# An FFT and mixture-of-experts kernel: scatters of the first segment 0.6 steps later, a scratch clear behind late scatters, and the routing copy on GpSimd

## The chip, the cores and the metric

The kernel runs on one core of a Trainium2 chip. The metric is the device time of one execution in microseconds (us); the time before is the median of three runs. Engine names are those of the profile: PE is TensorE's matmul, PEld its weight load, DVE is VectorE, ACT is ScalarE, POOL is GpSimd, SP is SyncE.

## The reference

The input x has 8 sequences of 2496 rows of 256 channels. Each channel of each sequence goes through a circular convolution, done in the frequency domain; then each of the 19,968 rows goes to the one of 8 experts whose gate logit is the largest, and comes back weighted with its gate probability.

```python
X = np.fft.rfft(x, axis=1)
Y = X * (filt_r + 1j * filt_i)[None]
x = np.fft.irfft(Y, n=2496, axis=1).reshape(8 * 2496, 256)
logits = x @ w_gate                          # 8 experts
expert_idx = np.argmax(logits, axis=1)
gate_w = softmax(logits)[arange(N), expert_idx]
for e in range(8):
    xe = x[expert_idx == e]
    h = np.maximum(xe @ w1[e], 0.0)          # 256 -> 1024
    out[expert_idx == e] = gate_w[...] * (h @ w2[e])   # 1024 -> 256
```

## The kernel before

The transform is done by matrix products. A sequence is two units of 128 channels, a unit is five steps: 80 steps in all. A step transposes (`spec1`), multiplies with a table (`spec2`), multiplies with the filter on DVE (`filt_`, tiles tr and ti), adds the two halves (`join`, on POOL up to step 70 and on DVE behind it) and multiplies back (`spec3`) into the buffer U.

When both units of a sequence b are through, the gate logits and the place of every row in its expert's list are worked out (`route1` to `route6`; the place is the tile dest, gate value and row number the tile meta). The rows are turned back into time in 11 pairs of groups of 117 rows: `inv1` and `inv2` make a tile yt of two groups by 260 columns. 256 of them are data, written by ACT (line 651); the last four are copied from meta by DVE (line 658, in `inv3`). Then POOL scatters each group into the list xs in HBM with one indirect DMA (line 158, in `scatter`). That makes 22 scatters a sequence, 176 in all. yt has five buffers.

The experts then work on blocks of 128 rows of xs, in three segments. The first has 16 blocks in 8 units and takes full blocks of the sequences up to b = 5, so it runs beside the last two sequences' inverse; the second has 48 blocks and waits for all scatters, and the rest is the third. A block b is loaded by SP (`load`), scaled and split into two f16 halves (`prep`, `split`), transposed by a DMA of SP (`turn`), and multiplied with both layers (`layer1`, `halves`, `layer2`, PE lines 1083 and 1109). ACT writes the result into ot (`out_`, four buffers), and POOL scatters it to the output (`send`, again line 158). At the end of the dispatch eight scatters of constant rows (`tail`) close the lists.

The order of the work on every engine is written out by hand. Each call is put into a list with a key in steps (`at`), the list is sorted by key, and the calls are made in that order; an engine does its instructions in the order in which they were made. A scatter has one of eight semaphores in turn, so it also waits until the scatter eight before it has landed. The key of `send` for a block of the first segment is 0.95 dx + 0.5 behind the start of the next block, where dx is the distance of two blocks: (90.5 - 80.9) / 16 = 0.6 steps.

Of the kernel before, what the change touches and what calls it, by code (L numbers as in the profile page):

```python
# [9 lines left out]
F32 = mybir.dt.float32  # L10
# [11 lines left out]
S, D, E, F = 2496, 256, 8, 1024  # L22
# [91 lines left out]
def tile_fft_moe(ctx, tc, x, filt_r, filt_i, w_gate, w1, w2, cst, out):  # L114
    nc = tc.nc
    B = x.shape[0]
# [7 lines left out]
    SEG = []  # L124
# [14 lines left out]
    cp = ctx.enter_context(tc.tile_pool(name="cp", bufs=1))  # L139
    ident = cp.tile([128, 128], F32, name="ident")  # L140
    small = cp.tile([128, 64], F32, name="small")
    zrow = cp.tile([128, ROW], F32, name="zrow")
    rbase = cp.tile([128, E], F32, name="rbase0")
    tbs = [cp.tile([128, 4], I32, name=f"tb{i}") for i in range(len(SEG))]
    nblk = cp.tile([128, 1], I32, name="nblk")
# [3 lines left out]
    def free(inst, own, *others):  # L149
        ins = inst.ins  # L150
        for g in (*others, own):
            tc.declare_no_dep(ins, group=g, reason="every row is written once")
        tc.add_to_no_dep_group(own, ins)
        writers.setdefault(own, []).append(ins.name)

    def scatter(dst, idx, src, bound, *groups):
        free(
            nc.gpsimd.indirect_dma_start(  # L158
                out=dst,
                out_offset=bass.IndirectOffsetOnAxis(ap=idx, axis=0),  # L160
                in_=src,
                in_offset=None,
                bounds_check=bound,
                oob_is_err=False,
            ),
            *groups,
        )

    def after(ins, names):
        for name in names:  # L170
            tc.add_manual_dep(
                ins,
                name,
                mybir.DependencyInfo(
                    mybir.DependencyClass.Sync, mybir.DependencyReason.DATA
                ),
                reason="the rows are dispatched",
            )
# [6 lines left out]
    with ExitStack() as fctx:  # L185
# [468 lines left out]
        def inv3(b, j, gg):  # L654
            yt = sti[b, j] if gg == 0 else sti.pop((b, j))
            dest, meta = rst[b]
            if gg == 0:
                nc.vector.tensor_copy(yt[:, :, D:], meta[:, 2 * j : 2 * j + 2])
            g = 2 * j + gg
            scatter(  # L660
                xs[:, :], dest[:, g : g + 1], yt[:, gg], E * NP - 1,
                f"s{b}", "ld", *(f"s{i}" for i in range(b)),
            )

        def blocks(rb, up, nm):

            t8 = lambda n, dt=F32: rp.tile([128, E], dt, name=nm + n, tag="t" + n)
            ci = t8("ci", I32)
            nb = t8("nb")
            nc.vector.tensor_tensor(nb, rb, small[:, 0:8], op=ALU.subtract)  # L670
            nc.vector.tensor_scalar(ci, nb, up, None, op0=ALU.add)
            nc.vector.tensor_scalar(ci, ci, 7, None, op0=ALU.arith_shift_right)
            nc.vector.tensor_copy(nb, ci)
            return nb
# [152 lines left out]
        def at(key, f, *a):  # L827
            work.append((key, f, a))
# [14 lines left out]
        def tail(e):  # L843
            scatter(
                xs[:, :], rst["tail"][:, e : e + 1], zrow, E * NP - 1,
                "z", "ld", *(f"s{i}" for i in range(B)),
            )


        K = {"s2": 1.394, "sr": 1.65, "si": 1.85, "s3": 3.6, "f": 0.063, "fd": 0.75, "w": 6.0, "wp": 4.1}  # L850
# [29 lines left out]
        for b in range(B):  # L880
# [26 lines left out]
            for j in range(NPAIR):  # L907
                z = s0 + lead + j * d
                at(z, inv1, b, j)
                at(z + 0.7 * c, inv2, b, j)  # L910
                z = max(z + 1.2 * c, s0 + c * RT[9] + 0.1 + 0.9 * d * j)
                for gg in range(2):
                    at(z + 0.45 * d * gg, inv3, b, j, gg)
# [9 lines left out]
            if b == B - 1:  # L923
                at(last + 0.1, tails)
                for e in range(E):
                    at(last + 1.2 + e, tail, e)
# [27 lines left out]
        home = []  # L954
# [173 lines left out]
        def send(b):  # L1128
            ot, t = st.pop(b)
            scatter(out[:, :], t, ot, N - 1, "out")  # L1130

# [33 lines left out]
        for b in range(NB):  # L1167
            z, d, s = tau[b]
            y = max(opened(s) + 0.3, z - (1.1 if b else 1.45))
            at(y, prep, b)  # L1170
            at(y + 0.05, split, b)
            at(y + 0.1, turn, b)
            at(z, layer1, b, 0)
            at(z + 0.2 * d, halves, b, 0)
            at(z + 0.25 * d, layer1, b, 1)
            at(z + 0.45 * d, halves, b, 1)
            nx, dx = (tau[b + 1][0], tau[b + 1][1]) if b + 1 < NB else (z + d, d)
            at(nx + 0.5 * dx, layer2, b, 0)
            at(nx + 0.75 * dx, layer2, b, 1)
            at(nx + 0.95 * dx, out_, b)  # L1180
            at(nx + 0.95 * dx + 0.5, send, b)
        for _, f, a in sorted(work, key=lambda w: w[0]):
            f(*a)

# [2 lines left out]
        with tc.If(n > NFIN - NREST):  # L1187
            for k in range(nu, len(units)):
                load(k)
                loadw(k, 0)  # L1190
                loadw(k, 1)
            for b in range(NB, NBLK):
                prep(b)
                split(b)
                turn(b)
            for b in range(NB, NBLK):
                for i in range(2):
                    layer1(b, i)
                    halves(b, i)
            for b in range(NB, NBLK):  # L1200
                layer2(b, 0)
                layer2(b, 1)
                out_(b)
                send(b)
# [32 lines left out]
```

## Time and profile before

| | |
|---|---|
| time, median of three runs | 1393.22 us (1393.07 to 1394.41) |
| time of the profiled execution | 1391.01 us |
| its span | 1389.2 us |
| PE busy | 1313.8 us (95%) |
| PEld busy | 1177.2 us (85%) |
| DVE busy | 831.5 us (60%) |
| ACT busy | 842.3 us (61%) |
| POOL busy | 470.7 us (34%) |

The span is what the profile shows between the first and the last instruction; 1.8 us of the profiled execution lie around it. Up to about 472 us the steps of the transform run, up to about 580 us the last two sequences are turned back beside the first segment, and behind about 608 us PE does expert blocks alone. A timeline row tells an instruction's start, its length, and in brackets how long its engine was idle before it and what ended that; "issue" means that the profile shows nothing that it waited for. The granted clock is given as a share of TensorE's full clock of 2.4 GHz; at 0.5 it is at its lower level of 1.2 GHz.

### The profile page before, as it was taken

Reading aid. Unit: us, or ns where it says so; the run is one execution under the profiler, and the core shown is the slowest. Engines: PE = TensorE matmul, PEld = TensorE weight load, DVE = VectorE, ACT = ScalarE, POOL = GpSimd, SP = SyncE. Lnnn points to the kernel's source line nnn. Section 1 sums busy time; section 2 is a strip of 40 time slices with the busy share of each in tenths; the row PEclk is TensorE's granted clock in tenths of the full one; section 3 lists DMA queues with packets and bytes.
Section 4 is the critical chain, followed back from the end, with each engine's and each line's share of the span. In section 5 each row is a group of like instructions: output and inputs, shape, how many; then the busy total and the mean of one; then the engine's idle time right before and its main releaser. Section 6 shows DMA issues by size and latency. Waiting matters only on the chain.

```text
span 1389.2 us, 38966 instructions
## 1 busy us (share of the span) xinstructions
PE 1313.8 (95%) x14855; PEld 1177.2 (85%) x14855; DVE 831.5 (60%) x2400; ACT 842.3 (61%) x1444; POOL 470.7 (34%) x446
## 2 busy tenths in 40 slices
PE   6799999999989899899999999999999999999997
PEld 5778777777877677789999999889999999999997
DVE  1698879888887464255555555555555555555552
ACT  3567667676766555455666665556656565656564
POOL 3638576485664433323111111111111111111111
PEclk9999999999999999999999999999999999999999
DMA  9746565565542722496878878573554546373731
GB/s 173 200 158 206 167 195 178 162 210 171 184 144 81 177 76 79 142 302 172 221 211 212 221 200 248 140 190 73 151 118 106 166 103 167 77 196 73 192 79 43
DMA packets 201438, 220.95 MB, mean 159 GB/s; under 512 B 104359, under 2 KB 177690, under 8 KB 190178
## 3 DMA queue, kind: packets, MB, share of 16 engines
q1 hardware_dynamic: 181310, 175.21, 45.9%
q0 software_dynamic: 19472, 42.51, 12.1%
q8 instruction: 118, 1.93, 0.6%
q10 hardware_dynamic: 468, 0.72, 0.2%
q14 instruction: 70, 0.57, 0.1%
HBM read 335.66 MB, written 61.56 MB: 286 GB/s over the span
## 4 chain that ended last, share of the span: by engine, by line
PE 48%; DMA 5%; issue 2%; DVE 1%; ACT 1%; SPq 1%; POOL 0%; POOLq 0%; ACTq 0%
PE ph L1083 24%; PE po L1109 24%; DMA wb<-wscr 3%; DMA wa<-wscr 1%; DVE bm L1097 1%; DMA T<-xs 0%; POOL out_dram L158 0%; ACT hs L1089 0%; ACT T L1091 0%; DMA xb<-xs 0%; DVE m L1048 0%; ACT xs L1062 0%; SPq L1070 0%; SPq L973 0%; DVE xs L1063 0%
## 5 line engine op out<-in xcount | busy, mean ns | idle before, releaser
L1083 PE MATMUL ph<-T,wa 128*128 128x128 f16 x7728 | 463.8, 220 | 14.1 <-issue 7.4
L1083 PEld LDWEIGHTS <-wa 128*128 128x128 f16 x7728 | 447.5, 98 | 27.2 <-issue 15.6
L1109 PE MATMUL po<-wb,T 128*128 128x256 f16 x2576 | 433.6, 274 | 6.6 <-DMA wb<-wscr 3.6
L1097 DVE TENSOR_TENSOR bm<-hs,T 128x512 f16<-128x512 f32 x322 | 222.7, 692 | 352.8 <-ACT T L1091 308.1
L158 POOL DMA_INDIRECT out_dram<-ot,t x161 | 157.2, 977 | 649.0 <-DVE xs L1063 567.1
L1109 PE MATMUL po<-wb,bm 128*128 128x256 f16 x1288 | 352.2, 273 | 0.0
L1109 PEld LDWEIGHTS <-T 128*128 128x128 f16 x2576 | 246.3, 98 | 38.2 <-issue 7.5
L1089 ACT ACTIVATE hs<-ph 128x512 f32<-128x512 f32 x322 | 191.6, 595 | 104.5 <-PE ph L1083 77.0
L158 POOL DMA_INDIRECT xs<-yt,dest x176 | 186.3, 1059 | 149.8 <-issue 45.7
L1062 ACT ACTIVATE xs<-xb,s 128x256 f16<-128x256 f32 x161 | 81.8, 508 | 226.3 <-DVE s L1052 224.0
L1091 ACT CAST T<-hs 128x512 f16<-128x512 f32 x322 | 199.0, 618 | 10.1
L1109 PEld LDWEIGHTS <-bm 128*128 128x128 f16 x1288 | 126.5, 98 | 15.2
L356 POOL TENSOR_TENSOR p<-tr,ti 128x512 f32<-128x512 f32 x71 | 95.4, 1344 | 85.2 <-DVE ti L348 78.3
L372 ACT COPY U<-pi 128x512 f32<-128x512 f32 (+1 forms) x80 | 87.4, 1093 | 48.9 <-PE pi L367 41.7
L1063 DVE SCALAR_TENSOR_TENSOR xs<-xb,s,xs 128x256 f16<-128x256 f32 x161 | 78.0, 485 | 59.3 <-ACT xs L1062 57.5
L649 PE MATMUL py<-gh,dm 117*117 117x512 f32 x176 | 94.0, 615 | 7.2 <-ACT gh L640 6.8
L367 PE MATMUL pi<-cm,p 128*128 128x128 f32 (+1 forms) x640 | 86.9, 279 | 10.3 <-POOL p L356 7.2
L264 PE MATMUL f<-a,x 117*128 117x117 f32 (+1 forms) x628 | 87.3, 277 | 5.6 <-DVE T L272 2.9
L327 PEld LDWEIGHTS px<-z,bm 128*128 128x128 f32 x640 | 80.0, 193 | 14.2 <-issue 11.5
L367 PEld LDWEIGHTS pi<-cm,p 128*128 128x128 f32 x640 | 79.0, 193 | 12.9 <-POOL p L356 7.9
L272 ACT COPY T<-f 128x468 f32<-128x468 f32 (+1 forms) x80 | 70.7, 884 | 30.5 <-PE f L264 28.8
L327 PE MATMUL px<-z,bm 128*128 128x128 f32 x640 | 87.1, 279 | 0.4 <-ACT U L372 0.4
(180 smaller groups left out, 1326.5 us busy)
## 6 DMA issues: line engine op xcount, KB each, us to landing
wb<-wscr SPq DMA_DIRECT2D x129, 1040.0 KB
wa<-wscr SPq DMA_DIRECT2D x129, 1024.0 KB
xb<-xs SPq DMA_DIRECT2D x161, 130.0 KB
wf<-in_moe_w_dram SPq DMA_DIRECT2D x32, 512.0 KB
x<-in_x_dram SPq DMA_DIRECT2D x210, 78.0 KB
wscr<-wh SPq DMA_DIRECT2D x8, 1040.0 KB
wscr<-wh SPq DMA_DIRECT2D x8, 1024.0 KB
xs<-yt,dest POOLq DMA_INDIRECT x176
```

Of the source, the lines that this page charges most:

```text
L158: nc.gpsimd.indirect_dma_start(out=dst, out_offset=bass.IndirectOffsetOnAxis(ap=idx, axis=0), in_=src, in_offset=None, bounds_check=bound, ...
L264: nc.tensor.matmul(ps[:, n : n + m], lhsT=xt.pop((u, g))[:m], rhs=a1[:m, :m], start=True, stop=True,)
L327: nc.tensor.matmul(ps[:, kk], lhsT=bm[:, 4 * it + kk], rhs=z[:, kk], start=True, stop=True,)
L356: e.tensor_tensor(p, tr, ti, op=ALU.add)
L367: nc.tensor.matmul(ps[:, o : o + n], lhsT=p[:, kk], rhs=cm[:, k, :n], start=True, stop=True)
L372: nc.scalar.copy(U[u % NU].rearrange("p n r -> p r n")[:, r0 : r0 + o // 64, :], ps[:, :o].rearrange("p (r n) -> p r n", n=N2),)
L649: nc.tensor.matmul(ps[:GP], lhsT=dm, rhs=gh[:GP], start=True, stop=True)
L1083: nc.tensor.matmul(ps[:, f], lhsT=w[:, p : p + 128], rhs=xt[:, r, c], start=(n == 0), stop=(n == 5))
L1089: nc.scalar.activation(s, ps, AF.Relu, scale=1.0 / B23)
L1091: nc.scalar.copy(hh, s)
L1097: nc.vector.tensor_tensor(hl, s, hh, op=ALU.subtract)
L1109: nc.tensor.matmul(ps, lhsT=h2[q][:, f % 4], rhs=wv[:, r, f], start=(f == 0 and n == 0), stop=(f == 7 and n == 2),)
```

## The change

A scratch tile `pad` of 128 x 384 f32 is added, and a function `pause` in which POOL clears it. It is called behind every scatter of the last two sequences (44), behind the eight scatters of `tail`, and behind the 16 scatters of the first segment's blocks: 68 times. The copy of the four routing columns into yt goes from DVE to POOL (88 times). The key of `send` for the first segment's blocks is 1.1 in place of 0.5, which is one block later.

```diff
--- before.py
+++ after.py
@@ -140,6 +140,7 @@
     ident = cp.tile([128, 128], F32, name="ident")
     small = cp.tile([128, 64], F32, name="small")
     zrow = cp.tile([128, ROW], F32, name="zrow")
+    pad = cp.tile([128, 384], F32, name="pad")
     rbase = cp.tile([128, E], F32, name="rbase0")
     tbs = [cp.tile([128, 4], I32, name=f"tb{i}") for i in range(len(SEG))]
     nblk = cp.tile([128, 1], I32, name="nblk")
@@ -165,6 +166,9 @@
             ),
             *groups,
         )
+
+    def pause():
+        nc.gpsimd.memset(pad, 0.0)
 
     def after(ins, names):
         for name in names:
@@ -655,12 +659,14 @@
             yt = sti[b, j] if gg == 0 else sti.pop((b, j))
             dest, meta = rst[b]
             if gg == 0:
-                nc.vector.tensor_copy(yt[:, :, D:], meta[:, 2 * j : 2 * j + 2])
+                nc.gpsimd.tensor_copy(yt[:, :, D:], meta[:, 2 * j : 2 * j + 2])
             g = 2 * j + gg
             scatter(
                 xs[:, :], dest[:, g : g + 1], yt[:, gg], E * NP - 1,
                 f"s{b}", "ld", *(f"s{i}" for i in range(b)),
             )
+            if b >= B - 2:
+                pause()
 
         def blocks(rb, up, nm):
 
@@ -845,6 +851,7 @@
                 xs[:, :], rst["tail"][:, e : e + 1], zrow, E * NP - 1,
                 "z", "ld", *(f"s{i}" for i in range(B)),
             )
+            pause()
 
 
         K = {"s2": 1.394, "sr": 1.65, "si": 1.85, "s3": 3.6, "f": 0.063, "fd": 0.75, "w": 6.0, "wp": 4.1}
@@ -1128,6 +1135,8 @@
         def send(b):
             ot, t = st.pop(b)
             scatter(out[:, :], t, ot, N - 1, "out")
+            if home[b][0] < SEG[0][2]:
+                pause()
 
 
 
@@ -1178,7 +1187,7 @@
             at(nx + 0.5 * dx, layer2, b, 0)
             at(nx + 0.75 * dx, layer2, b, 1)
             at(nx + 0.95 * dx, out_, b)
-            at(nx + 0.95 * dx + 0.5, send, b)
+            at(nx + 0.95 * dx + (1.1 if home[b][0] < SEG[0][2] else 0.5), send, b)
         for _, f, a in sorted(work, key=lambda w: w[0]):
             f(*a)
```

PE, ACT and SP have the same instructions in the same order. DVE loses the 88 copies and keeps the order of the rest. On POOL 88 copies and 68 clears are added, and the output scatters stand elsewhere. The line numbers of the changed kernel are 1 to 9 higher.

POOL, where the sequence b = 6 begins to be scattered (yt6_0 is its first pair of groups, xs_57 the list in HBM). Before:

```order
L568 MEMSET meta6_5103 117x88
L158 DMA xs_57<-yt6_0_5121,dest6_5170 161792x260 x2
L158 DMA xs_57<-yt6_1_5174,dest6_5170 161792x260 x2
L158 DMA xs_57<-yt6_2_5210,dest6_5170 161792x260 x2
L158 DMA xs_57<-yt6_3_5257,dest6_5170 161792x260 x2
L158 DMA xs_57<-yt6_4_5300,dest6_5170 161792x260 x2
```

Now:

```order
L572 MEMSET meta6_5104 117x88
L662 COPY yt6_0_5122<-meta6_5104 117x2x4
L159 DMA xs_57<-yt6_0_5122,dest6_5171 161792x260
L171 MEMSET pad_65 128x384
L159 DMA xs_57<-yt6_0_5122,dest6_5171 161792x260
L171 MEMSET pad_65 128x384
L662 COPY yt6_1_5175<-meta6_5104 117x2x4
L159 DMA xs_57<-yt6_1_5175,dest6_5171 161792x260
L171 MEMSET pad_65 128x384
L159 DMA xs_57<-yt6_1_5175,dest6_5171 161792x260
L171 MEMSET pad_65 128x384
```

Each scatter (a row with x2 is two of them) has a clear of pad behind it, and each pair a copy from meta before it.

POOL, where the first results of the first segment go out (ot0 is the first block's), between the end of sequence 6 and the beginning of sequence 7. Before:

```order
L568 MEMSET meta7_5868 117x88
L158 DMA out_0_dram<-ot0_5744,t0_5395 19968x256
L158 DMA xs_57<-yt6_9_5748,dest6_5170 161792x260 x2
L158 DMA out_0_dram<-ot1_5905,t1_5465 19968x256
L158 DMA xs_57<-yt6_10_5952,dest6_5170 161792x260
L158 DMA xs_57<-yt7_0_5990,dest7_6059 161792x260 x2
L158 DMA xs_57<-yt6_10_5952,dest6_5170 161792x260
L158 DMA out_0_dram<-ot2_6052,t2_5530 19968x256
```

Now:

```order
L572 MEMSET meta7_5887 117x88
L662 COPY yt6_9_5766<-meta6_5104 117x2x4
L159 DMA xs_57<-yt6_9_5766,dest6_5171 161792x260
L171 MEMSET pad_65 128x384
L159 DMA xs_57<-yt6_9_5766,dest6_5171 161792x260
L171 MEMSET pad_65 128x384
L159 DMA out_0_dram<-ot0_5762,t0_5406 19968x256
L171 MEMSET pad_65 128x384
L662 COPY yt6_10_5969<-meta6_5104 117x2x4
L159 DMA xs_57<-yt6_10_5969,dest6_5171 161792x260
L171 MEMSET pad_65 128x384
L662 COPY yt7_0_6007<-meta7_5887 117x2x4
```

The scatter of ot0 stood before the pair yt6_9 and stands behind it; that of ot1 (five rows further than the last one shown here) stood before yt6_10 and stands behind yt7_0 and yt6_10.

DVE, in the third sequence. Before:

```order
L658 COPY yt2_2_2463<-meta2_2303 117x2x4
L346 TENSOR_TENSOR tr36_2517<-px36_2498,ff_129 128x512
L347 TENSOR_TENSOR ti36_2518<-px36_2498,ff_129 64x512
L348 TENSOR_TENSOR ti36_2518<-px36_2498,ff_129 64x512
L272 COPY T0_113<-f1_8_4_2542 128x12x39
L658 COPY yt2_3_2515<-meta2_2303 117x2x4
L346 TENSOR_TENSOR tr37_2581<-px37_2560,ff_129 128x512
L347 TENSOR_TENSOR ti37_2582<-px37_2560,ff_129 64x512
```

Now:

```order
L350 TENSOR_TENSOR tr36_2518<-px36_2499,ff_130 128x512
L351 TENSOR_TENSOR ti36_2519<-px36_2499,ff_130 64x512
L352 TENSOR_TENSOR ti36_2519<-px36_2499,ff_130 64x512
L276 COPY T0_114<-f1_8_4_2543 128x12x39
L350 TENSOR_TENSOR tr37_2582<-px37_2561,ff_130 128x512
L351 TENSOR_TENSOR ti37_2583<-px37_2561,ff_130 64x512
```

The copies are gone, and nothing else has moved.

## Rows read from the trace of the kernel before

**Rows 1.** Windows: stretch, us, busy of PE, PEld, DVE, ACT, POOL, granted clock, DMA.

```profile
456.00:470.20 14.20, 9.31 (x55) 7.04 (x54) 8.85 (x29) 6.82 (x11) 7.09 (x8) 0.76 0.55 163
516.10:524.90 8.80, 5.03 (x27) 3.11 (x25) 1.20 (x6) 3.14 (x7) 3.41 (x4) 0.81 0.20 63
556.40:562.40 6.00, 3.55 (x33) 2.90 (x31) 0.35 (x1) 2.65 (x5) 1.92 (x2) 0.72 0.40 111
568.40:576.00 7.60, 4.72 (x33) 3.35 (x31) 1.24 (x3) 2.75 (x6) 2.13 (x3) 0.78 0.53 177
470.20:516.10 45.90, 44.92 (x526) 37.23 (x524) 26.36 (x120) 26.75 (x51) 15.51 (x17) 1.00 0.55 124
225.00:243.00 18.00, 17.69 (x123) 14.57 (x124) 16.42 (x25) 12.89 (x20) 14.85 (x14) 1.00 0.76 229
650.00:675.00 25.00, 24.93 (x346) 23.64 (x345) 13.72 (x50) 14.76 (x28) 5.83 (x6) 1.00 0.96 255
60.00:400.00 340.00, 322.22 (x2434) 265.53 (x2432) 292.93 (x576) 239.40 (x352) 204.88 (x181) 1.00 0.58 183
```

**Rows 2.** Timeline, PE, 515 to 523: start, us, engine, line, operation [idle before].

```profile
518.11 0.22 PE L1083 MATMUL ph<-T,wa 128*128 128x128 f16 x1 [1.21 <-issue]
...
518.82 0.23 PE L1083 MATMUL ph<-T,wa 128*128 128x128 f16 x1 [0.50 <-issue]
```

**Rows 3.** Timeline, POOL: first and last scatter of three runs.

```profile
446.52 0.99 POOL L158 DMA_INDIRECT xs<-yt,dest  x1 [16.32 <-ACT gh L640]
...
462.24 0.99 POOL L158 DMA_INDIRECT xs<-yt,dest  x1 [0.30 <-issue]
...
511.65 0.99 POOL L158 DMA_INDIRECT xs<-yt,dest  x1 [3.42 <-DMA xs<-yt,dest]
...
519.42 1.00 POOL L158 DMA_INDIRECT xs<-yt,dest  x1 [0.30 <-issue]
...
563.67 1.00 POOL L158 DMA_INDIRECT xs<-yt,dest  x1 [5.04 <-ACT hs L1089]
...
570.15 0.99 POOL L158 DMA_INDIRECT out_dram<-ot,t  x1 [0.30 <-issue]
```

**Rows 4.** Timeline, PE and DVE, around 457 to 465.

```profile
457.89 1.06 PE L327 MATMUL px<-z,bm 128*128 128x128 f32 x8
...
464.54 0.69 DVE L346 TENSOR_TENSOR tr<-px,ff 128x512 f32<-128x512 f32 x1 [4.42 <-PE pi L367]
```

**Rows 5.** Timeline, ACT, DVE and POOL: one image tile, its routing columns, its scatter.

```profile
485.04 0.58 ACT L651 COPY yt<-py 117x512 f32<-117x512 f32 x1 [0.39 <-PE py L649]
...
493.29 0.17 DVE L658 COPY yt<-meta 117x8 f32<-117x8 f32 x1
...
494.31 1.00 POOL L158 DMA_INDIRECT xs<-yt,dest  x1 [7.96 <-ACT ot L1125]
```

**Rows 6.** Timeline, POOL, 224 to 243: scatters and joins.

```profile
225.98 1.30 POOL L356 TENSOR_TENSOR p<-tr,ti 128x512 f32<-128x512 f32 x1
227.47 1.00 POOL L158 DMA_INDIRECT xs<-yt,dest  x1 [0.20 <-DVE yt L658]
...
240.93 0.99 POOL L158 DMA_INDIRECT xs<-yt,dest  x1 [0.31 <-issue]
...
241.93 1.29 POOL L356 TENSOR_TENSOR p<-tr,ti 128x512 f32<-128x512 f32 x1
```

**Rows 7.** Groups by line, and timeline of DVE: the routing copy.

```profile
L658 DVE COPY yt<-meta 117x8 f32<-117x8 f32 x88 | 28.6, 331 | 0.5
...
236.26 1.90 DVE L658 COPY yt<-meta 117x8 f32<-117x8 f32 x1
```

**Rows 8.** Groups by line: operations of POOL near the added ones.

```profile
L568 POOL MEMSET meta<- 117x88 f32 x8 | 1.5, 186 | 0.0
...
L809 POOL MEMSET go<- 128x176 f32 x1 | 0.2, 236 | 0.0
...
L356 POOL TENSOR_TENSOR p<-tr,ti 128x512 f32<-128x512 f32 x71 | 95.4, 1344 | 85.2 <-DVE ti L348 78.3 <-PE px L327 6.0
```

## The prediction, made before the changed kernel was run

> **What bounds the kernel now.** I read the busy time in windows first, then the gaps of PE with the timeline, then POOL's timeline beside them. PE is busy 95% of the span, its order does not change, and where only expert blocks run it loses nothing: 24.93 of 25 us at full clock [rows 1]. So only PE's gaps can be won. The reader is to see that they are not spread evenly. Beside the last two sequences there are four stretches in which PE is idle 4.89 us (14.20 - 9.31), 3.77, 2.45 and 2.88 us, and in which the granted clock falls to a mean of 0.76, 0.81, 0.72 and 0.78, that is, for a part of each to the lower of its two levels, and it falls where PE stands still. Between the first two, PE loses 0.98 us in 45.9 [rows 1].
>
> What ends these gaps is no semaphore that the profile names. In the second stretch PE starts one instruction about every 0.7 us, in the middle of a tile whose operands are there: gaps of 1.21 and 0.50 us "<-issue" [rows 2]. In the first the news of finished work comes late: the matmuls px start at 457.89 and take 1.06 us, and DVE, which waits for them, goes on at 464.54 [rows 4].
>
> Beside this stands POOL. The four stretches lie in or right behind the long unbroken rows of scatters that it has behind 440 us: 12 from 446.52 to 462.24 (one every 1.43 us), 7 from 511.65 to 519.42 (1.30 us), 6 from 563.67 to 570.15 (1.30 us) [rows 3], and six more like the last, which end in the third stretch. PE is hit some 5 us behind the beginning of a row at 1.30 us (516.1 against 511.65, 568.4 against 563.67) and some 10 us behind the beginning of the one at 1.43 us (456 against 446.52). Earlier, POOL scatters as many, but with joins between: nine from 227.47 to 240.93, one every 1.68 us [rows 6], and PE is busy 17.69 of 18 us there, at full clock [rows 1]. So I take it that scatters closer than some 1.5 us for more than 5 to 10 us hold PE up. Which resource it is, no row tells.
>
> **The change part by part.** *The clears.* Between two scatters POOL is idle 0.30 us, behind a join 0.20 us, and an operation begins at once behind a scatter [rows 6]. A clear of m us between two scatters thus puts them m - 0.10 us further apart. The trace has clears of 88 and 176 columns, 0.186 and 0.236 us [rows 8], which is 0.57 ns a column; for 384 columns that makes an estimate of 0.35 us (bounds: 0.24 us, the longer of the two rows, and 1.03 us, the same row taken in proportion to the columns). Two scatters then begin 0.99 + 0.35 + 0.20 = 1.54 us apart.
>
> *The copies on POOL.* Not in the trace. Below stands the clear of 88 columns, 0.19 us, above the join of 512 columns with two inputs, 1.34 us [rows 8]. Eight columns are nearest to the former, and I take 0.25 us. A pair then takes 2 x 1.54 + 0.25 = 3.33 us, one scatter every 1.67 us; with an output scatter between, 3 x 1.54 + 0.25 = 4.87 us for three, every 1.62 us. That is the pace of the stretch which does PE no harm. POOL's load grows by 68 x 0.25 = 17 us and 88 x 0.15 = 13 us; it is busy 15.51 of 45.9 us in the late part [rows 1], so there it has the room.
>
> *The copies off DVE.* 28.6 us of DVE, 0.331 us each, go away [rows 7]. Most take 0.17 us [rows 5], but one that meets a join of POOL takes 1.90 us [rows 7]. DVE is busy 292.93 of 340 us while the transform runs, and PE is idle 340 - 322.22 = 17.8 us there [rows 1]. That idle time is the upper bound of the gain; the lower is nothing, since ACT hides some of it. DVE's load falls by less than a tenth, so I take 1 us. More matters late: yt was written by ACT at 485.04, the copy on DVE came at 493.29, and the scatter at 494.31 [rows 5]. Here POOL waited 8 us for 0.17 us of work that stood behind other work in DVE's order. Without this, scatters follow ACT's tiles one by one and pile up less, which breaks the rows a second time.
>
> *The later output scatters.* When POOL comes sooner, an output scatter in the old place could make it wait for ot, with the scatters of yt queued behind it. One block later this wait is covered. An ot is written again four blocks later; its scatter now stands about 1.8 blocks behind the writing (1.1 / 0.6), so two blocks are left for the landing. I count nothing for it; without the cover POOL would wait, and PE only once all five yt are full. PE, ACT and SP keep their order, so no load stands elsewhere.
>
> *The sum.* Idle in the four stretches: 4.89 + 3.77 + 2.45 + 2.88 = 14.0 us. Clock: (1 - 0.76) x 14.20 + 0.19 x 8.80 + 0.28 x 6.00 + 0.22 x 7.60 = 8.4 us. The first stretch holds 8.3 us of these 22.4, the others 14.1. The first one's row had the pace nearest to the harmless one, and the new pace of 1.67 us has little to spare against 1.68, so I count two thirds of it, 5.5 us. What PE loses anyhow, 2.1% of 36.6 us by the stretch between them, is 0.8 us. 14.1 + 5.5 - 0.8 + 1 = 19.8 us. The profiled execution took 1391.0 us, so it would take 1371.2; the median of the runs is 2.2 us above it, which gives 1373 us. The next thing that is late is then the tile gh of ACT before py, and the loads of the second segment.
>
> A page speaks against this. The Trainium skill, SBUF — State Buffer, section "SBUF: two separate sides", says that transfers and engines reach the memory by different ports and cannot hold each other up; by this alone scatters would not slow PE, whatever their pace. That is the first rival below. The rows speak for a connection, but by its time alone: all the rows of six or more behind 440 us have a stretch beside them.
>
> **The rivals.** *The scatters' pace is not the cause.* For it: the first segment's blocks, with their loads of weights and their transposes, run in the same time, and "issue" names nobody. Against it: the same transfers run beside every expert block, where PE loses 0.07 us in 25 [rows 1]. Then only the 1 us of DVE is won: 1392 us.
>
> *The pace is the cause, but 1.6 us is not enough.* The stretches come later and are shorter. If half of the 22.4 us goes, 1393.2 - 11 - 1 = 1381 us; this lies between 1381 and 1389.
>
> *The copies make POOL late, and the kernel slower.* While the transform runs, POOL is busy 14.85 of 18 us, and its idle time is mostly the 0.2 or 0.3 us between instructions [rows 1, 6]. If a copy takes as long as a join, 1.34 us (for instance because it waits for operations of DVE), 11 copies a sequence put POOL 11 x 1.24 = 13.7 us back. A join stands 1.75 steps ahead of the `spec3` that reads it (keys 1.85 and 3.6), and a step takes 5.32 us (three between the joins at 225.98 and 241.93 [rows 6]), so 9.3 us are hidden; 4.4 us for each of the six sequences with joins on POOL are not, 26 us in all. With a fall of the clock at each, at 1.7 us as in the later stretches, it is 36 us. Less the 20 us won: 1399 to 1409 us. It decides from 9.3 / 11 + 0.10 = 0.95 us a copy. Against it stands how short operations of few columns are in rows 8. A page bears on it: the Trainium skill, SBUF — State Buffer, "Who interferes with whom", has an operation of GpSimd that reads wait for a running operation of DVE with two inputs in the memory, and a copy on DVE wait for GpSimd; the 1.90 us beside a join agree with the second half, and what the first would cost, no run here shows yet.
>
> **How the numbers follow.** The stretches go, whole or nearly so: 0.60, between 1364 (all of them, and 5 us in the transform) and 1381 us. A part stays: 0.15, 1381 to 1389. Not the cause: 0.12, 1389 to 1395. POOL late: 0.13, 1396 to 1409. The range from 1364 to 1391 us holds the first two and a part of the third, about 0.8. Within 0.2% of 1393.22 us, about what a measurement of this kernel can tell from no change, is 1390.4 to 1396.0: 0.11. Faster: 0.60 + 0.15 + 0.01 = 0.76. Slower: 0.13.
>
> **What would show it.** In the profile after: no single matmuls 0.7 us apart between 440 and 580 us, and a granted clock of 1.00 there; scatters of the last two sequences 1.54 us or more apart, and none waiting for DVE's copy; a clear of about 0.35 us and a copy of about 0.25 us; expert blocks alone some 20 us sooner, with all behind them as before. I am wrong if stretches stand in spite of a pace of 1.6 us, if they go but PE waits for ACT or DVE for as long, or if a copy on POOL takes a microsecond.

## The result: 1372.45 us, and a second measurement of the same step

| | before | after | ratio (95%) |
|---|---|---|---|
| first measurement, 5 runs each | 1393.07 us (1389.91 to 1394.41) | 1372.45 us (1369.06 to 1381.67) | 0.987 [0.9848, 0.9891] |
| second measurement (below, `a_again`) | 1391.39 us (17 runs) | 1372.94 us (1371.02 to 1378.05, 5 runs) | 0.9866 [0.9842, 0.989] |
| predicted | | 1373 us, 1364 to 1391 | |

The profiled execution of the first measurement is the slowest of its five (1381.67 us; span 1379.6). So the second measurement's profiles of both kernels, from one chip, are read beside it: 1394.52 us before (span 1392.6) and 1373.33 us after (span 1371.2).

First the windows, in the columns of [rows 1]. This is the first profile of the kernel after:

```profile
472.00:486.00 14.00, 10.65 (x93) 7.45 (x91) 4.26 (x17) 6.93 (x12) 11.67 (x20) 0.76 1.03 310
486.00:520.00 34.00, 33.17 (x378) 27.97 (x379) 21.67 (x96) 19.07 (x37) 14.64 (x22) 1.00 0.26 65
520.00:570.00 50.00, 50.00 (x588) 43.47 (x587) 24.71 (x101) 33.14 (x62) 41.80 (x64) 1.00 0.49 134
```

The second profile of the kernel before, and then that of the kernel after:

```profile
440.00:472.00 32.00, 25.98 (x175) 21.15 (x174) 24.41 (x66) 18.51 (x29) 14.86 (x14) 0.89 0.37 117
515.00:526.00 11.00, 6.69 (x59) 5.00 (x57) 3.84 (x22) 2.81 (x6) 5.66 (x6) 0.83 0.31 90
555.00:580.00 25.00, 19.79 (x172) 14.26 (x170) 8.12 (x33) 10.21 (x20) 10.66 (x11) 0.87 0.42 122
440.00:600.00 160.00, 141.13 (x1419) 115.55 (x1418) 81.73 (x312) 84.75 (x154) 61.91 (x61) 0.93 0.43 121
```

```profile
440.00:472.00 32.00, 30.15 (x238) 24.85 (x235) 25.18 (x58) 22.86 (x36) 19.19 (x32) 1.00 0.40 107
515.00:526.00 11.00, 11.00 (x130) 9.87 (x129) 8.38 (x42) 7.41 (x15) 9.49 (x16) 1.00 0.44 118
555.00:580.00 25.00, 21.76 (x279) 19.56 (x276) 11.10 (x39) 13.54 (x26) 15.77 (x23) 1.00 0.92 221
440.00:600.00 160.00, 150.85 (x1706) 130.13 (x1704) 92.79 (x331) 99.14 (x179) 98.91 (x150) 1.00 0.60 158
```

The second profile of before has the stretches of [rows 1] again, at nearly the same places. After, they are gone: from 486 to 570 us PE is idle 0.83 us in the first profile, and in the second it does 130 matmuls from 515 to 526 us in place of 59. In 440 to 600 us it does 1706 in place of 1419. The DMA columns rise with it (121 to 158 GB/s). By the profile's list of PE's waits in 440 to 600 us, 12.1 and 10.1 us of idle time are "<-issue" in the two profiles of before, none and 0.4 us in those of after. Up to 570 us one fall of the clock is left in the first profile of after: from 472 to 486 us PE is idle 3.35 us, nearly all of it for the transposed rows of a block, and the mean clock is 0.76.

How much the stage gave is read from one matmul group at either end of it, in PE's timeline. In the first pair of profiles, before and after:

```profile
454.67 1.02 PE L649 MATMUL py<-gh,dm 117*117 117x512 f32 x2
...
650.36 2.84 PE L1083 MATMUL ph<-T,wa 128*128 128x128 f16 x48
```

```profile
460.82 1.02 PE L653 MATMUL py<-gh,dm 117*117 117x512 f32 x2
...
638.31 2.84 PE L1090 MATMUL ph<-T,wa 128*128 128x128 f16 x48
```

In the second pair, before and after:

```profile
452.66 1.02 PE L649 MATMUL py<-gh,dm 117*117 117x512 f32 x2
...
649.09 2.84 PE L1083 MATMUL ph<-T,wa 128*128 128x128 f16 x48
```

```profile
454.95 1.02 PE L653 MATMUL py<-gh,dm 117*117 117x512 f32 x2
...
628.30 2.84 PE L1090 MATMUL ph<-T,wa 128*128 128x128 f16 x48
```

These are the same instructions, since PE's order is unchanged. In the first pair the kernel after is 6.15 us late when it comes into the stage and 12.05 us early behind it: 18.2 us won there. In the second it is 2.29 us late and then 20.79 us early: 23.1 us. My term for the stage was 18.8 us (14.1 + 5.5 - 0.8).

POOL in the second profile of after, against [rows 3]:

```profile
452.00 1.03 POOL L159 DMA_INDIRECT xs<-yt,dest  x1 [0.18 <-issue]
453.02 0.44 POOL L171 MEMSET pad<- 128x384 f32 x1
453.39 0.21 POOL L662 COPY yt<-meta 117x8 f32<-117x8 f32 x1
453.90 1.01 POOL L159 DMA_INDIRECT xs<-yt,dest  x1 [0.30 <-POOL yt L662]
454.91 0.43 POOL L171 MEMSET pad<- 128x384 f32 x1
455.52 0.99 POOL L159 DMA_INDIRECT xs<-yt,dest  x1 [0.18 <-issue]
...
460.49 0.62 POOL L662 COPY yt<-meta 117x8 f32<-117x8 f32 x1
```

Two scatters stand 1.62 us apart inside a pair (453.90 to 455.52) and 1.90 us from one pair to the next (452.00 to 453.90), where 1.54 and 1.79 us were expected. The groups by line of the first profile of after say the same:

```profile
L171 POOL MEMSET pad<- 128x384 f32 x68 | 29.7, 437 | 0.1
L662 POOL COPY yt<-meta 117x8 f32<-117x8 f32 x88 | 28.3, 321 | 14.4 <-DVE meta L590 12.7 <-DVE sa L608 1.6
```

What is late in the stage now, in PE's timeline of the second profile of after:

```profile
474.28 1.51 PE L1090 MATMUL ph<-T,wa 128*128 128x128 f16 x24 [2.43 <-DMA T<-xs]
...
580.60 1.61 PE L1090 MATMUL ph<-T,wa 128*128 128x128 f16 x26 [3.06 <-ACT xs L1069]
```

Both are waits with a named releaser: in the first the DMA that transposes a block's rows, in the second ACT's scaling of such rows.

### The profile page after: what moved, and what is told of

The parts are those of the page before. It is cut to its first block, busy times and chain, and to the rows that moved or that the text cites. A ratio compares the mean times of both kernels' runs of the same rounds, so it can differ in the third digit from the quotient of the medians.

```text
span 1379.6 us, 39050 instructions
## 1 busy us (share of the span) xinstructions
PE 1316.1 (95%) x14855; PEld 1181.7 (86%) x14855; DVE 813.9 (59%) x2312; ACT 846.0 (61%) x1444; POOL 524.7 (38%) x602
## 3 DMA queue, kind: packets, MB, share of 16 engines
q8 instruction: 118, 1.93, 0.6%
## 4 chain that ended last, share of the span: by engine, by line
PE 76%; DMA 8%; DVE 8%; issue 3%; ACT 2%; SPq 1%; POOL 1%; POOLq 0%; DVEq 0%; ACTq 0%
PE ph L1090 27%; PE po L1116 26%; PE py L653 5%; PE f L268 4%; PE pi L371 4%; PE px L331 4%; DMA wa<-wscr 2%; PE pg L638 2%; DMA wb<-wscr 2%; PE pt L316 2%; DMA U<-in_x_dram 2%; PE plw L502 2%; DMA xb<-xs 1%; DVE wm L404 1%; DVE ti L351 1%
```

## The experiments

Theory P is that of the prediction: scatters too close together, for too long, hold PE up, and the clears cure it by the distance that they make. Theory D is that DVE's late copy piles the scatters up, so that moving the copy is what helps. The letters of later theories are explained where they are expected. Four sets of runs fell on four chips; each kernel is compared with the kernel before on its own chip.

### First chip: the change in parts, and nothing to cure

`e1_copies` is the kernel before with one edit:

```diff
-                nc.vector.tensor_copy(yt[:, :, D:], meta[:, 2 * j : 2 * j + 2])
+                nc.gpsimd.tensor_copy(yt[:, :, D:], meta[:, 2 * j : 2 * j + 2])
```

> The kernel before with one edit: the routing copy is on GpSimd. No clears, output scatters in their old place. Theory P (scatters closer than about 1.5 us for more than 5 to 10 us hold TensorE up): a copy and the wait for it (0.2 to 0.5 + 0.3 us by the changed kernel's profile) between pairs widen the pace to about 1.5 us and the scatters no longer pile up behind VectorE, so the stretch at 460 us stays in part and the three later ones mostly go: 10 to 16 us faster than before, 1377 to 1383 us. Theory D (the gain is that scatters and image tiles no longer wait for VectorE; the pace does not matter): the whole gain, 20 us, 1372 to 1374 us.

`e2_clears` is the kernel before with `pad`, `pause` and its three calls, and neither the copies nor the key of `send`.

> The kernel before with one edit: the 68 clears on GpSimd. The routing copy stays on VectorE and the output scatters in their old place. Theory P: the pace is 1.62 us (0.99 + 0.44 + 0.18), so all four stretches go although scatters still wait for VectorE: 16 to 21 us faster, 1372 to 1377 us, no single matmuls 0.7 us apart. Theory D: no gain, 1391 to 1394 us, and the stretches stand.

`e3_clears_copies` is the kernel after with the old key:

```diff
-            at(nx + 0.95 * dx + (1.1 if home[b][0] < SEG[0][2] else 0.5), send, b)
+            at(nx + 0.95 * dx + 0.5, send, b)
```

> The changed kernel without the later output scatters (key 0.5 again); clears and the copy on GpSimd stay. By the prediction the later place only covers a wait of GpSimd that TensorE does not feel: within 2 us of the changed kernel, 1371 to 1375 us. The rival: an output scatter that waits for ot holds the scatters of yt up until all five yt are full, 3 to 8 us slower than the changed kernel, 1375 to 1380 us.

`e4_copies_sends` is the kernel after without the clears:

```diff
     def pause():
-        nc.gpsimd.memset(pad, 0.0)
+        pass
```

> The changed kernel without its 68 clears; the copy on GpSimd and the later output scatters stay. Theory P: the pace is 1.30 us inside a pair and about 1.5 us on the whole, near the limit: part of the first stretch is back, 4 to 10 us slower than the changed kernel, 1376 to 1383 us. Theory D: the clears do nothing, 1371 to 1374 us.

Measured (12 runs each; the kernel before 1367.85 us, 1359.23 to 1374.27, in 35 runs):

| | us | ratio (95%) |
|---|---|---|
| e1_copies | 1369.51 | 1.0009 [0.9991, 1.0027] |
| e2_clears | 1366.65 | 0.9993 [0.9974, 1.0011] |
| e3_clears_copies | 1368.69 | 1.0011 [0.999, 1.0031] |
| e4_copies_sends | 1372.94 | 1.0026 [1.0009, 1.0044] |

Both theories missed. No part gained anything: on this chip the kernel *before* already took 1367.85 us, 25 us less than in the first measurement. It was not traced here; of the four parts, the window of e1_copies shows how little there was to win:

```profile
440.00:600.00 160.00, 149.96 (x1679) 130.15 (x1678) 89.58 (x325) 97.85 (x176) 73.20 (x87) 0.98 0.58 157
```

It has no clears, and PE still does 1679 matmuls here, nearly as many as the kernel after. From 510 to 530 us it is never idle. The list of PE's waits in 440 to 600 us has no "<-issue" in any of the four traces, and between the two matmuls of the second pair above the stage takes 173.5 to 177.2 us in them, where it takes 196.4 us in the second profile of before and 173.3 in that of after. So either the pace had never been the cause, or this chip (or the chip at that time) bears a pace that the one of the first measurement did not. The next step had to be the two kernels unchanged, and a dose.

### Second chip: both kernels unchanged, and more scatters

`b_again` is the kernel before and `a_again` the kernel after, unchanged.

> The kernel before, unchanged, for a second profile of it. Theory C (the four stretches belong to the chip or the session in which the first measurement was made, not to the kernel alone): where its time is again near 1368 us, its profile shows no matmuls some 0.7 us apart between 440 and 580 us, although it has the same unbroken rows of scatters at 1.30 us; PE's idle time there is made of waits for the transposing DMA, as in the four kernels before this. Theory P (scatters closer than 1.5 us hold PE up, wherever the kernel runs): the stretches stand at the same rows, about 14 us idle and 8 us of lowered clock, and the time is 20 us above that of the kernel after beside it.

> The kernel after, unchanged. Theory C: where the kernel before takes about 1368 us, ratio 0.997 to 1.005 (the three partial versions gave 1.0009, 0.9993, 1.0011 and 1.0026); where the kernel before takes about 1393 us, ratio 0.985 to 0.989 again. Theory P: ratio 0.985 to 0.989 in both cases.

`d1_more` adds 22 scatters to the kernel before:

```diff
+    xd = dram.tile([NROWS, ROW], F32, name="xd")
...
                 f"s{b}", "ld", *(f"s{i}" for i in range(b)),
             )
+            if b >= B - 2 and gg:
+                scatter(xd[:, :], dest[:, g : g + 1], yt[:, gg], E * NP - 1, "d", "ld")
```

> The kernel before with 22 more scatters: the second group of every pair of the last two sequences is scattered a second time at once, into a list of its own in HBM that nobody reads. Rows of scatters at 1.30 us become half as long again (the row of 12 becomes one of about 18, that of 7 one of about 10), and POOL has 22 x 1.30 = 29 us more work there. Theory P: more or longer stretches than the 22 us of the first profile of before, so a ratio of 1.01 to 1.03. Theory C, on a chip where the kernel before takes about 1368 us: no matmuls 0.7 us apart, ratio 0.998 to 1.006 (only what POOL's later scatters cost in waits for yt).

Measured, with the kernel before at 1391.39 us (1387.62 to 1396.74): b_again 1394.03 us, ratio 1.001 [0.9995, 1.0026]; a_again 1372.94 us, 0.9866 [0.9842, 0.989]; d1_more 1420.38 us, 1.0218 [1.0188, 1.0249]. The stretches and the gain are back, and more scatters make it worse by 29 us, in the middle of what theory P expected. The 22 scatters are also 29 us of work for POOL; but that PE waits for a late POOL is not what the trace names. Of PE's idle time in 440 to 600 us, 29.7 us are "<-issue" (10.1 in b_again), and 2.2 us name another cause. PE's timeline of d1_more shows the two forms that a hold-up takes, single instructions and late news of finished work:

```profile
478.77 2.06 PE L650 MATMUL py<-gh,dm 117*117 117x512 f32 x2 [9.07 <-issue]
...
530.83 0.22 PE L1086 MATMUL ph<-T,wa 128*128 128x128 f16 x1 [0.35 <-issue]
532.26 0.22 PE L1086 MATMUL ph<-T,wa 128*128 128x128 f16 x1 [1.22 <-issue]
```

In the first row PE begins as soon as the tile gh is there, 9.07 us after it stood still at 469.70. ACT makes gh from a tile that PE had finished by then, but only at 478.13; until then ACT is idle but for one copy of 0.58 us, as its timeline shows ("remote" is a release whose sender the profile does not name):

```profile
478.13 0.59 ACT L641 COPY gh<-pg 117x512 f32<-117x512 f32 x1 [3.03 <-remote]
```

DVE is late too. It goes on at 472.39 with the tile px, which PE had finished at 462.66:

```profile
472.39 0.69 DVE L347 TENSOR_TENSOR tr<-px,ff 128x512 f32<-128x512 f32 x1 [8.58 <-remote]
```

This is [rows 4] again, longer.

### Third chip: the parts again, and the pace in doses

`f_copies` is e1_copies, and `f_clears` is e2_clears; `d2_more` is d1_more. `h_small` is f_clears with a shorter clear:

```diff
-    pad = cp.tile([128, 384], F32, name="pad")
+    pad = cp.tile([128, 88], F32, name="pad")
```

> The kernel before with the copies on GpSimd and nothing else, a second time. Where the kernel before takes about 1391 us: theory P (pace) has a pair at 1.30 + 0.5 us for the copy, one scatter every 1.56 us, so most of the stretches go: ratio 0.987 to 0.992. Theory B (the number of scatters close together decides, and only a clear behind every one keeps them apart): 1.30 us inside the pairs is still too close, ratio 0.994 to 1.000. Where the kernel before takes about 1368 us both give 0.997 to 1.004, as the first time (1.0009).

> The kernel before with the 68 clears and nothing else, a second time. Where the kernel before takes about 1391 us: theory P expects one scatter every 1.62 us and no stretch, ratio 0.985 to 0.990. Theory D (DVE's late copies pile the scatters up, and the clears only add work): 0.996 to 1.002. Where the kernel before takes about 1368 us both give 0.997 to 1.003, as the first time (0.9993).

> The same 68 clears on 88 columns in place of 384: about 0.19 us each, one scatter every 1.36 us in place of 1.30 and 1.62. Where the kernel before takes about 1391 us, theory P expects that the stretches begin later and are shorter, but stay: ratio 0.992 to 0.999. Theory T (any instruction between two scatters is enough, whatever its length): as the long clears, 0.985 to 0.990. Where the kernel before takes about 1368 us: 0.998 to 1.002.

> The kernel before with 22 more scatters, a second time, for the chip that it falls on. Where the kernel before takes about 1368 us: if that chip only stands more of them (theory P with another threshold), stretches of matmuls 0.7 us apart appear, and the time is 1385 us or more; if it has no such effect (theory C), none appear, and the time is 1366 to 1378 us with unbroken rows at 1.30 us in the trace. Where the kernel before takes about 1391 us: 1415 to 1428 us as the first time.

The kernel before took 1391.64 us here (1386.71 to 1396.36, 16 runs); it was not traced here, and its two profiles from above stand in the table. The pace is measured alike in every trace: the mean step in all rows of six or more scatters from 440 to 600 us, where a row ends when the next scatter begins 1.9 us later or more. Steps that nothing delays are shorter, some 1.30 us in before and 1.31 and 1.50 in turn in f_copies; the other two are shown below. The column of PE's idle time leaves out the waits that name a late tile (for gh they are 12.8 us in d2_more, 4.4 in f_copies, 3.7 in h_small and 0.2 in f_clears). The stage is the time between the two matmuls of the second pair above, in one profile of each.

| | one scatter every | PE idle "<-issue", 440 to 600 us | stage | us | ratio (95%) |
|---|---|---|---|---|---|
| d2_more, 22 more | 1.33 us, longer rows | 14.0 us | 216.2 us | 1417.38 (one run) | 1417.38 / 1391.64 = 1.0185, no interval |
| before | 1.36 and 1.34 us | 12.1 and 10.1 us | 193.9 and 196.4 us | 1391.64 | 1 |
| f_copies | 1.40 us | 2.9 us | 184.3 us | 1385.48 | 0.9958 [0.9937, 0.9979] |
| h_small | 1.40 us | 6.8 us | 187.8 us | 1384.12 | 0.9954 [0.9939, 0.997] |
| f_clears | 1.64 us | 0.2 us | 175.7 us | 1372.85 | 0.987 [0.9841, 0.99] |

POOL in h_small, and then in f_clears:

```profile
453.77 0.99 POOL L159 DMA_INDIRECT xs<-yt,dest  x1 [0.18 <-issue]
454.77 0.18 POOL L171 MEMSET pad<- 128x88 f32 x1
455.14 0.99 POOL L159 DMA_INDIRECT xs<-yt,dest  x1 [0.18 <-issue]
```

```profile
449.20 0.99 POOL L159 DMA_INDIRECT xs<-yt,dest  x1 [0.18 <-ACT gh L644]
450.19 0.44 POOL L171 MEMSET pad<- 128x384 f32 x1
450.81 0.99 POOL L159 DMA_INDIRECT xs<-yt,dest  x1 [0.18 <-DVE yt L662]
```

PE in the second stretch, in the same order:

```profile
510.00:530.00 20.00, 18.00 (x186) 13.85 (x184) 12.67 (x69) 10.85 (x22) 12.63 (x21) 1.00 0.35 96
```

```profile
510.00:530.00 20.00, 19.83 (x221) 16.72 (x219) 12.89 (x61) 12.51 (x24) 16.40 (x22) 1.00 0.39 104
```

f_copies and h_small are different edits: one moves the copy and clears nothing, the other clears and leaves the copy on DVE. They come to the same mean pace, and to the same third of the gain. f_clears comes near the pace of the kernel after (1.71 us in both of its profiles), and to its whole gain, with the copies on DVE and the output scatters in their old place. So on this chip it is the pace; theory D fails (it expected 0.996 or more of f_clears), and so does theory T, for which any instruction between two scatters would do. My expectation of theory P for f_copies (0.987 to 0.992) was missed, because I had the copy add 0.5 us to a pair. It takes the place of 0.30 us of idle time, and adds 0.20 (449.97 to 450.47 holds the copy and the idle time behind it). That 1.40 us fits theory P is said after the fact. Theory B, that 1.30 us inside the pairs is still too close, had the right range (0.994 to 1.000). h_small, with a clear behind every scatter, ends at the same ratio as f_copies at the same mean pace; but the distances inside a pair, 1.31 and 1.37 us, are close to each other too, so the mean pace and the shortest distance are not told apart here.

The chip's part is seen by the same kernel on two chips. POOL's timeline of f_copies on the third chip, and of e1_copies on the first:

```profile
453.28 1.00 POOL L158 DMA_INDIRECT xs<-yt,dest  x1 [0.30 <-issue]
454.59 0.99 POOL L158 DMA_INDIRECT xs<-yt,dest  x1 [0.30 <-issue]
455.57 0.21 POOL L658 COPY yt<-meta 117x8 f32<-117x8 f32 x1
456.08 1.00 POOL L158 DMA_INDIRECT xs<-yt,dest  x1 [0.30 <-issue]
```

```profile
453.55 1.00 POOL L158 DMA_INDIRECT xs<-yt,dest  x1 [0.30 <-POOL yt L658]
454.86 0.99 POOL L158 DMA_INDIRECT xs<-yt,dest  x1 [0.30 <-ACT gh L640]
455.85 0.20 POOL L658 COPY yt<-meta 117x8 f32<-117x8 f32 x1
456.36 1.00 POOL L158 DMA_INDIRECT xs<-yt,dest  x1 [0.30 <-POOL yt L658]
```

They scatter alike to a few hundredths, and the second stretch lies beside a row of 7 scatters on the third chip and of 10 on the first, one every 1.39 us in both (512.12 to 520.48 and 507.49 to 519.97). And PE, in windows of f_copies:

```profile
455.00:473.00 18.00, 12.86 (x87) 10.16 (x86) 9.26 (x28) 8.40 (x14) 11.78 (x17) 0.81 0.57 166
510.00:530.00 20.00, 18.07 (x201) 14.97 (x200) 11.35 (x57) 10.02 (x21) 11.37 (x14) 1.00 0.38 103
```

and of e1_copies:

```profile
455.00:473.00 18.00, 13.10 (x116) 10.53 (x116) 11.74 (x36) 12.18 (x20) 13.12 (x18) 0.97 0.74 181
510.00:530.00 20.00, 20.00 (x236) 17.43 (x234) 12.78 (x64) 12.76 (x25) 13.83 (x18) 1.00 0.42 115
```

The third chip loses 1.93 us of 20 in the second window, the first none; in the first window the one has 87 matmuls at a clock of 0.81, the other 116 at 0.97. (The first chip's idle time there is the wait for a transposed block, as in the kernel after.) I found nothing else in the traces by which the chips differ. Whether the first chip would show stretches with more scatters was not seen: d2_more fell on the third. Each chip was used at one time only, so the chip and the time of its runs are not told apart either.

### Fourth chip: what is late next

`g_load` is the kernel after with the loads of the first segment's blocks earlier on SP:

```diff
-            at(max(opened(s), z - 2.0, PLACE[0] - 1.95), load, k)
+            at(max(opened(s), z - (2.0 if s else 2.6), PLACE[0] - 1.95), load, k)
```

> The kernel after, with the loads of the first segment's blocks 0.6 steps earlier in the order (2.6 steps ahead of the block in place of 2.0), so that on SP they stand ahead of a transposing DMA that waits for DVE, and ahead of 1 MB of weights. It aims at what is late in the kernel after: layer 1 of the second unit waits 2.43 us for a transposed block (471.85 to 474.28 in its second profile), whose rows DVE got only at 473.09. If the load's place in the order sets this, the wait goes, and a fall of the clock behind it: 2 to 5 us less than the kernel after, a ratio of 0.983 to 0.986 where the kernel before takes about 1391 us, and of 0.996 to 1.000 where it takes about 1368 us. If the rows come late for another reason (the weights before them in the queues), or if the next wait takes its place, the ratio is that of the kernel after, 0.987, or 1.001 to 1.003.

Measured: 1372.67 us (1366.7 to 1375.2, 5 runs), the kernel before 1394.43 us; ratio 0.9846 [0.9825, 0.9867]. PE's timeline and the window of g_load:

```profile
468.81 1.40 PE L1090 MATMUL ph<-T,wa 128*128 128x128 f16 x22 [0.64 <-DMA T<-xs]
```

```profile
440.00:600.00 160.00, 155.41 (x1784) 135.06 (x1783) 93.94 (x337) 101.70 (x184) 103.35 (x154) 1.00 0.62 171
```

The wait of 2.43 us went down to 0.64. PE does 78 matmuls more in the window than in the second profile of the kernel after, in part because it comes into the stage 3.5 us sooner. Between the two matmuls of the second pair the stage takes 169.1 us in place of 173.3, in one profile of each, and that of g_load is the fastest of its five executions. So the place of the load set that wait. As a time of the kernel it is not shown: the interval overlaps that of the kernel after (0.9866 [0.9842, 0.989]), which was measured on another chip.

## Why the prediction was right, step by step

*PE bounds the kernel, and the four stretches are what can be won.* Right in both pairs of profiles. The stage gave 18.2 and 23.1 us, where 18.8 was the term. That they lie so close is in part luck. The sum takes the loss by the lowered clock over the whole length of each stretch, PE's idle time included. Over PE's busy time alone it is 0.24 x 9.31 + 0.19 x 5.03 + 0.28 x 3.55 + 0.22 x 4.72 = 5.2 us and not 8.4, and the four stretches then hold 19.2 us and not 22.4. By the prediction's own steps the term is then some 16 us (12.1 + 4.7 - 0.8), and the stage gave more in both pairs.

*The scatters' pace holds PE up.* This rested on time alone when it was predicted, and the prediction gave it 0.60. The doses show it now: at 1.34 us with longer rows 2.2% slower, at 1.40 us 0.4 to 0.5% faster, at 1.64 us 1.3% faster. The bound of "some 1.5 us" held in so far as stretches stand at 1.40 and none at 1.64; where between them it lies is open. The rival that the pace is not the cause is out on the second and third chip. On the first chip things went just as that rival says (1.0009 and 0.9993 for the parts). The prediction had no place for chips that differ, and this is its gap: the gain of 20 us belongs to the kernel and a chip (or the time of its runs), not to the kernel alone.

*The rule that spoke against.* The Trainium skill, SBUF — State Buffer, section "SBUF: two separate sides", lets transfers and engines reach the memory without holding each other up. On the first chip e1_copies agrees with it: PE has no idle time "<-issue" there. The doses on the second and third do not, if the rule is read as "scatters cannot slow PE". But what the rows show there is instructions that start late and news that comes late, not operations that take longer, so the memory's ports need not be the place.

*Two thirds of the first stretch, 5.5 us.* Too cautious, and made up by a wait that I had not named. At 1.6 us and more no stretch is left there, but the second unit's block waits for its transposed rows, 3.29 us in the first profile of after (in the window from 472 to 486 us, with the fall of the clock) and 2.43 in the second. So the sign "a granted clock of 1.00" held in the second profile and not in the first. I had named gh before py and the loads of the second segment as late next; it was the transposing DMA of the first segment, and behind it the load (g_load).

*The clear, 0.35 us.* It took 0.437 us, inside the bounds of 0.24 and 1.03. Scatters with a clear between them are 0.99 + 0.44 + 0.18 = 1.61 us apart, not 1.54. The error went the good way.

*The copy on POOL, 0.25 us.* 0.321 us in the mean, so the rival of a late POOL, which needed 0.95 us, did not come. In the second profile of after 67 of the 88 copies take 0.18 to 0.22 us. The other 21 take 0.34 to 1.22 us, five of them more than the microsecond that I had named as a sign of being wrong, all five while the transform runs. Each of the 21 overlaps an operation of DVE with two inputs, so they fit the rule cited there: the copy of 0.62 us at 460.49 runs beside this operation of DVE with two inputs, in DVE's timeline of the second profile of after,

```profile
460.37 0.69 DVE L360 TENSOR_TENSOR p<-tr,ti 128x512 f32<-128x512 f32 x1
```

and ends 0.05 us behind it. That is what the Trainium skill, SBUF — State Buffer, "Who interferes with whom", says of an operation of GpSimd that reads beside one of DVE with two inputs. Its price is 0.4 us here and 1.0 us at most, and POOL has the room.

*DVE's relief, 1 us in the transform.* Not seen. DVE's busy time in 60 to 400 us fell as it should, from 292.93 [rows 1] to 274.12 us in the first profile of after, but the kernel came into the late stage 6.15 and 2.29 us later than before. Part of that is PE's clock. From 200 to 300 us it is 1.00 in the first profile of before, 0.97 in the second of before and in both of after; from 300 to 440 us it is 0.99 and 0.98 before and 0.95 in both of after. That the copies on POOL lower it is not shown: f_copies has them too, and 0.98 in both windows. And f_clears, with the copies on DVE, takes as long as the kernel after. So the relief is worth nothing that can be measured here.

*The copies off DVE break the rows.* Failed as a reason of its own: by the pace that they make, the copies are worth 0.4% alone, and beside the clears nothing. [Rows 5] bear the reading that POOL waited for DVE only in part: the profile names ACT's tile ot, which this scatter does not read, and the scatter begins 0.85 us behind the end of the copy. In any case the scatters that pile up hurt by their pace.

*The later output scatters, nothing.* Nothing was found. e1_copies and e4_copies_sends differ in the key alone, on one chip: 1.0009 [0.9991, 1.0027] with the old one and 1.0026 [1.0009, 1.0044] with the new one, intervals that overlap. On a chip with stretches, f_clears has the old key (and the copies on DVE), and the same ratio as the kernel after.

What stays open is which resource the scatters hold, and what the first chip has, always or at that time, that the others lack.

## What to carry to other kernels

Where a bound engine starts single instructions some 0.7 us apart "<-issue" in the middle of a tile, look at what else runs in that time, and change its pace by two different edits that have nothing else in common; if both give the same, that speaks for the pace, and an edit that makes it worse tests it from the other side. An operation that nobody needs, of less than half a microsecond, was worth 1.3% here when it stood between indirect DMAs. Before parts of a change are measured, run both kernels unchanged on the chip at hand: a gain may need a chip that has the trouble.

## What the runs showed of the hardware that was not expected

The same kernel took 1367.85 us on one chip and 1391.39, 1391.64 and 1394.43 us on three others. Stretches stand in traces from the second and third chip and from the first measurement, and in none of the four traces of the first chip; on the fourth only g_load was traced, which has none. In a stretch PE starts one pair of weight load and matmul every 0.7 us or so, while POOL goes on with a scatter every 1.30 us. In the second profile of before the pairs start at 519.23, 519.95 (of this one only the weight load is recorded), 520.67, 521.37, 522.09 and 522.82, beside scatters at 518.60, 519.89 and 521.18. At the milder pace of f_copies the step is the same, but it carries more: 1, 3, 5 and 2 matmuls from 517.85, 518.56, 519.29 and 520.03. Whether DVE is slowed likewise is open: in the second profile of before it has no operation in the stretch, and those just ahead follow each other at 0.07 to 0.2 us. An indirect DMA leaves POOL idle 0.30 us before the next one, and 0.18 us when a clear stands between, so that a clear of 0.19 us costs only 0.07 us of pace.
